# Reordering the opening, the weight sums and the q scalings of a retention and two-layer kernel

## The chip, the cores and the metric

The kernel runs on one core of a Trainium2 chip. The metric is the device time of one execution in microseconds (us).

## The reference

Retention with a decaying state, then two dense layers with an activation between them; the reference, cut to its core:

```python
# B, H, S, D = 4, 8, 768, 64; d_model 512, d_ff 2048
gamma = 1.0 - 2.0 ** (-5.0 - np.arange(H))
for t in range(S):
    state = gamma[None, :, None, None] * state + np.einsum('bhd,bhe->bhde', k[:, :, t], v[:, :, t])
    y[:, :, t] = scale * np.einsum('bhd,bhde->bhe', q[:, :, t], state)
x = y.transpose(0, 2, 1, 3).reshape(B * S, H * D)
h = x @ w_in
out = (h * np.tanh(softplus(h))) @ w_out
```

## The kernel before, in words

**Tiling.** The tokens of each batch are cut into chunks of 128, 24 in all (numbered over the batches). Inside a chunk retention is done by matrix products: scores of k against q, a triangular mask, the masked scores times v, and q times the state that the chunk before left; the state itself is the sum of the outer products of k and v, with a decay. q and v are scaled by powers of gamma when they are turned to fp16 (`qs`, `vs`).

**Blocks.** The dense layers work on blocks of chunks: the first block has four (chunks 0 to 3), each later one two. `first_block` does the retention of chunks 0 to 3 in fp16, whose x goes straight into the first layer (`first_g1` for the first four of 16 groups of d_ff, `g1` for the other twelve), and then calls `first_g2`, the second layer of block 0. `first_g2` also prepares chunks 4 to 7: it scales q and v (`cast_q`, `cast_v` on POOL), loads k as fp16 through POOL's DMA queue (`bring_k`), transposes q and k (`turn` on TensorE for chunks 4 and 5, `turn_by_dma` through SP's DMA queue from chunk 6 on), and does the scores, masks and state of block 1's chunks 4 and 5.

From block 1 on both layers are done with seven products in place of eight (`g1_seven`, `seven`): that needs sums of the weights. `win_sums` makes those of the input weights (`wsum`, two lots `a` of eight DVE additions each), `weight_sums` those of the output weights (`tmat`, two halves of four additions each), `g_sum` those of the activations of block 0 (`gsum`). Weight sums that are not done at once wait in the list `late`; `some_late(n)` issues the next n of them on DVE.

**Weights.** Both weight matrices are loaded as fp32 in four slices each (`wi`, `wt`) and cast to fp16: `cast_win(slice, half, engine)` and `cast_wout`. The table `plan` in `first_block` says after which of the groups 4 to 15 of the first layer which cast or sum is issued. `mish` is the activation, on ACT, which reads a group's PSUM tile and frees it; four of the tiles rotate under the tag `mm` (two others, tag `at`, hold scores, y and groups 8 and 9).

**Order.** The program is written out by hand: each engine runs its instructions in the order of the code, and semaphores hold it until what it reads is there. `gate(x)` is a one-column POOL copy that makes the POOL work behind it wait for x. `steps_of_first` is the table for block 1: what is issued between which of its products.

**Names and lines that the prediction uses.** L249 q of the first chunks; L288 `cast_two` of v on POOL; L204 and L206 `cast_win` on ACT and on POOL or DVE; L214 and L216 `cast_wout` on ACT and DVE; L314 `scores_half`; L321 `mask_half`; L333 `outer_first`; L343 and L345 `state_first` (matmul with the identity, then the multiplication on DVE); L374 `present_first`; L381 `past_first`; L386 `xt_out`; L1057 `first_g1`; L687 `g1`; L703 `mish`; L770 `win_sums`; L722 to L725 `weight_sums`; L406 `cast_q`; L418 `bring_k`; L423 `cast_v`; L427 `gate`; L431 `turn_by_dma`; L453 and L455 `turn`; L604 `outer_fifth`; L614 `decay_of_fifth`; L497 `scores_two`; L1242, L1247 and L1281 copies and additions of outputs in `first_g2`.

Of the kernel before, what the change touches and what calls it, by code (L numbers as in the profile page):

```python
# [11 lines left out]
AF = mybir.ActivationFunctionType  # L12
# [4 lines left out]
def kernel(  # L17
# [125 lines left out]
    nload, late, early = [0], [], set()  # L143
    BRING = CPB
    stores = []
    last_ended, yet = [], []

# [49 lines left out]
    def cast_win(s, half, eng):  # L199
        src = wtmps["in", s]  # L200
        t = cpool.tile([P, NBP, TB // 2], FP16, name=f"win{s}_{half}")
        src = src[:, :, half * (TB // 2):(half + 1) * (TB // 2)]
        if eng is nc.scalar:
            nc.scalar.copy(t, src)  # L204
        else:
            eng.tensor_copy(t, src)  # L206
        wins[s, half] = t
# [190 lines left out]
    def by_head(g, t):  # L398
        if g < NCH:
            return t.rearrange("p (x j) d -> p x j d", x=2)  # L400
        return t.rearrange("p (j x) d -> p x j d", x=2)

    def cast_q(g):
        if g < NCK:
            f = qs.rearrange("p (x j) -> p x j", x=2).unsqueeze(3)
            nc.gpsimd.tensor_tensor(  # L406
                by_head(g, room16(g)[0]), by_head(0, loaded[g][0]),
                f.broadcast_to((P, 2, HP, D)), op=ALU.mult)
# [40 lines left out]
    def turn(g, on_act=False):  # L449
        q16, k16 = cast[g][:2]  # L450
        t_ps = atps.tile([P, H, C], FP16, name="t_ps", tag="at")
        for i in range(HP):
            nc.tensor.transpose(t_ps[:, i], q16[:, 2 * i:2 * i + 2], ident)  # L453
        for i in range(HP):
            nc.tensor.transpose(t_ps[:, HP + i], k16[:, 2 * i:2 * i + 2], ident)  # L455
        qkt = qktp.tile([P, H, C], FP16, name="qkt", bufs=4)
        if on_act:
            nc.scalar.copy(qkt, t_ps)
        else:
            nc.vector.tensor_copy(qkt, t_ps)  # L460
        qkts[g] = (qkt[:, :HP], qkt[:, HP:])
# [599 lines left out]
    def first_block():  # L1061
# [50 lines left out]
        for half in range(2):  # L1112
            cast_two("v", 1, half)
        cast_win(0, 0, nc.gpsimd)
        at = at_tile()
        scores_half(1, 1, at)
        mask_half(1, 1, at)
        y = [atps.tile([P, 2, HP, C], FP32, name="y_ps", tag="at")[:, 0] for _ in range(2)]
        outer_first(1, [0])
        state_first(2)  # L1120
        h_ps = [mmps.tile([P, 1, TB], FP32, name="h_ps", tag="mm") for _ in range(2)]
        for u in range(2):
# [1 line left out]
        present_first(1, y, range(HP))  # L1124
        past_first(2, y)
        past_first(3, y)
        cast_win(0, 1, nc.vector)
        xt_out_by_two(2, y)
        for u in range(2, FPS):
            h_ps.append(mmps.tile([P, 1, TB], FP32, name="h_ps", tag="mm"))  # L1130
# [13 lines left out]

        def more_sums():
            late.extend(win_sums(1))
            some_late(8)
            late.extend(weight_sums(0) + weight_sums(1))

        plan = {6: [(cast_win, NSL - 1, 0, nc.scalar)],  # L1150
                7: [(cast_win, NSL - 1, 1, nc.scalar), (more_sums,)],
                9: [(cast_wout, 0, slice(0, 3)), (cast_wout, 0, slice(3, 4), True), (room_for_more,),
                    (bring_first,)],
                10: [(some_late, 1)],
# [30 lines left out]
    def first_g2():  # L1185
# [33 lines left out]
        for p in pairs:  # L1219
            mm(pe[p], sm(p, 1), t(1), True)  # L1220
            nc.scalar.copy(m5[p], pe[p])
        cast_wout(2, slice(0, 2))
        cast_wout(2, slice(2, 4), True)
        some_late(1)
        gate(tmats[0][:, 1, 0, :1])
        cast_q(CPB)
        cast_q(CPB + 1)
        cast_v(CPB)
        some_late(1)
# [10 lines left out]
        for p in pairs:  # L1240
            mm(px[p], sm(p, 2), t(2))
            nc.scalar.copy(osb[p][0][:, 1], px[p])  # L1242
        mm(pe[0], sm(0, 4), b(2, 1))
        turn(CPB, True)
        for p in pairs:
            mm(px[p], sm(p, 3), t(3))
# [14 lines left out]
        scores(CPB + 1)  # L1261
        mask(CPB)
        mask(CPB + 1)
        some_late(2)
        for p in pairs:
            mm(px[p], a(p, 1, 2), t(4))
        cast_v(CPB + 2)
        bring_k(CPB + 3)
        cast_q(CPB + 2)
        turn_by_dma(CPB + 2)  # L1270
        load_early_v(CPB + 4)

        def end(p, i, half):
            for f in range(2 * half, 2 * half + 2):
# [20 lines left out]
        for p, i in ends:  # L1295
            if (p, i) == (0, 1):
                y_two(1)
            end(p, i, 1)
            if (p, i) == (0, 1):
                midway_of_seventh(CPB + 2)  # L1300
            if p == 0:
                ended(p, i)
            if (p, i) == ends[0]:
                some_late(1)
        x_sums(FIRST, lambda: state_sum(CPB + 2))
        last_ended.extend(ends[2:])
        last_ended.append(ended)
# [54 lines left out]
    def steps_of_first(blk):  # L1362
        a, nb = first[blk] + 4, blk + 1
        A, B = slice(0, FPS), slice(FPS, 2 * FPS)
        return {
            "at1": [(gate_x, blk), (cast_q, a - 1), (decay_next, a - 2), (bring_k, a)],
            "at2": [(turn_by_dma, a - 1), (load_to, a + 2), (cast_v, a - 1), (cast_v, a), (bring_k, a + 1)],
            "at3": [(end_first,), (load_to, a + 3)],
            "at5": [(store, 2), (sums_a, blk, A)],
            "g7": [(sums_a, blk, B)],  # L1370
            "m1": [(scores_and_outer, a - 1), (state_midway, a - 1), (state_sum, a - 1),
                   (decay_next, a - 1)],
            "m5": [(sums_b, blk), (gate_g, blk), (mask_two, nb), (cast_q, a), (turn_by_dma, a),
                   ],
            "m2": [(sums_c, blk), (gate_s, blk), (cast_q, a + 1), (turn_by_dma, a + 1),
                   (load_to, a + 4), (store, 2)],
            "m7": [(y_of, nb), (state_midway, a), (state_sum, a), (decay_next, a)],
            "m3": [(y_end,), (bring_k, a + 2)],
            "m4": [(x_sums, nb)],
        }  # L1380
# [38 lines left out]
```

## Time and profile before

| | us |
|---|---|
| median of 3 runs | 190.89 (190.85 to 191.61) |
| the profiled execution | 190.88 |
| its span in the trace | 189.0 |

The profiled execution's own time is 1.88 us longer than its span: what lies around the first and last instruction. Engines are named PE (TensorE matmul), PEld (its weight loads), DVE (VectorE), ACT (ScalarE), POOL (GpSimd), SP (SyncE, which here only issues DMAs). A row of the timeline has the start and the length in us, the engine, the line of the kernel, the operation, the tile written and the tile read, the size and the number of instructions merged in the row; in brackets, the idle time before it and what ended it. A matmul's end is modelled, and rows of pipelined instructions overlap. The stages by the timeline: the opening with retention of chunks 0 to 3 up to about 20 us, the first layer of block 0 to about 30.6 us, its second layer with the retention of chunks 4 and 5 to about 47 us, then ten blocks of two chunks of some 14 us each, and the last stores.

### The profile page before, as it was taken

What the parts mean: (1) busy time and instruction counts of PE and PEld (TensorE: products, weight loads), DVE (VectorE), ACT (ScalarE), POOL (GpSimd) and SP (SyncE); (2) the same over time, 40 slices, a digit from 0 to 9 for tenths busy, and PEclk for the clock granted to TensorE, in tenths of its full rate; (3) what the DMA queues carried; (4) which work ended last, traced back from release to release, by engine and by line L of the source; (5) the groups of instructions that cost most, each with busy time, mean ns of one, the idle gap of its engine ahead of it and who ended that gap; (6) DMA issues with size and microseconds to landing.
All of it is one profiled execution on the core that took longest, in us unless ns stands there. A gap on an engine that the chain in (4) does not pass through costs nothing.

```text
span 189.0 us, 7724 instructions
## 1 busy us (share of the span) xinstructions
PE 182.5 (97%) x3283; PEld 155.8 (82%) x3283; DVE 155.6 (82%) x329; ACT 126.8 (67%) x249; POOL 95.3 (50%) x135
## 2 busy tenths in 40 slices
PE   7789999999999999999999999999999999999992
PEld 3457546975988988988988988988988989989981
DVE  3997899879899699797897897797897897796662
ACT  3462599385883983983983984974874974965960
POOL 6570107696878937924935925916916913000000
PEclk9999999999999999999999999999999999999999
DMA  5999999999999999999998995999996984300203
GB/s 165 351 368 405 404 407 279 278 248 134 151 192 251 180 285 210 208 219 177 167 194 146 188 187 158 197 195 120 178 203 117 148 144 59 114 0 17 101 0 111
DMA packets 95521, 36.17 MB, mean 191 GB/s; under 512 B 82560, under 2 KB 88960, under 8 KB 95488
## 3 DMA queue, kind: packets, MB, share of 16 engines
q1 hardware_dynamic: 74112, 32.78, 75.3%
q0 software_dynamic: 21088, 2.62, 22.4%
q8 instruction: 25, 0.41, 0.9%
q10 hardware_dynamic: 288, 0.30, 0.4%
q14 instruction: 8, 0.07, 0.1%
HBM read 27.30 MB, written 6.29 MB: 178 GB/s over the span
## 4 chain that ended last, share of the span: by engine, by line
PE 91%; DVE 3%; DMA 2%; POOL 1%; issue 1%; ACT 0%; SPq 0%; DVEq 0%; POOLq 0%
PE h_ps L820 34%; PE o_ps L956 32%; PE h_ps L687 6%; PE o_ps L1210 5%; DMA qfirst<-in_q_dram 2%; PE h_ps L1057 2%; PE o_ps L1275 2%; PE y_ps L532 2%; PE u_ps L483 2%; PE at L497 2%; DVE am L321 2%; PE y_ps L543 2%; POOL qfirst L249 1%; DVE osb L977 1%; PE at L314 0%
## 5 line engine op out<-in xcount | busy, mean ns | idle before, releaser
L840 DVE TENSOR_TENSOR hsum<-h_ps,hsnap 128x512 f32<-128x512 f32 x60 | 38.5, 685 | 10.1 <-ACT hsnap L830 6.6
L830 ACT COPY hsnap<-h_ps 128x512 f32<-128x512 f32 x60 | 32.1, 589 | 10.3 <-PE h_ps L820 10.1
L820 PEld LDWEIGHTS <-wsum 128*128 128x128 f16 x640 | 36.2, 98 | 0.1
L835 ACT ACTIVATE g<-hsum 128x512 f16<-128x512 f32 x60 | 34.6, 643 | 0.6 <-DVE hsum L840 0.2
L956 PEld LDWEIGHTS <-gsum 128*128 128x128 f16 x320 | 30.4, 98 | 3.7
L820 PE MATMUL h_ps<-xsum,wsum 128*128 128x128 f16 x480 | 30.2, 220 | 0.0
L956 PE MATMUL o_ps<-tmat,gsum 128*128 128x256 f16 x240 | 29.5, 273 | 0.0
L820 PEld LDWEIGHTS <-win 128*128 128x128 f16 x480 | 28.2, 98 | 0.9
L418 POOL DMA_DIRECT2D qk<-in_k_dram x36 | 27.5, 777 | 0.0
L956 PEld LDWEIGHTS <-g 128*128 128x128 f16 x248 | 22.7, 98 | 2.6
L406 POOL TENSOR_TENSOR qk<-qf,qvs 128x512 f16<-128x512 f32 x20 | 22.1, 1106 | 0.0
L956 PE MATMUL o_ps<-wout,g 128*128 128x256 f16 (+1 forms) x168 | 20.8, 268 | 0.0
L423 POOL TENSOR_TENSOR v<-vf,qvs 128x512 f16<-128x512 f32 x20 | 20.7, 1060 | 0.0
L820 PE MATMUL h_ps<-xt,win 128*128 128x128 f16 x320 | 19.6, 220 | 0.0
L550 ACT COPY hsum<-y_ps 128x512 f32<-128x512 f32 x9 | 5.3, 585 | 18.3 <-PE y_ps L543 18.3
L977 DVE TENSOR_TENSOR osb<-o_ps,snap 128x256 f32<-128x256 f32 (+1 forms) x32 | 13.0, 413 | 5.0 <-PE o_ps L956 2.4
L597 POOL TENSOR_TENSOR stc<-suc,gcv 128x256 f16<-128x256 f32 x15 | 9.9, 662 | 13.6 <-DVE suc L592 13.6
L427 POOL COPY gate<-gsum 128x1 f16<-128x1 f16 x10 | 1.9, 186 | 26.8 <-DVE gsum L927 26.8
L965 ACT COPY snap<-o_ps 128x256 f32<-128x256 f32 x31 | 11.4, 371 | 5.4 <-PE o_ps L956 5.0
L820 PE MATMUL h_ps<-xsum,win 128*128 128x128 f16 x160 | 12.3, 220 | 0.0
L820 PE MATMUL h_ps<-xt,wsum 128*128 128x128 f16 x160 | 12.2, 220 | 0.0
L835 ACT ACTIVATE g<-h_ps 128x512 f16<-128x512 f32 x20 | 12.0, 599 | 0.0
(144 smaller groups left out, 309.4 us busy)
## 6 DMA issues: line engine op xcount, KB each, us to landing
vf<-in_v_dram SPq DMA_DIRECT2D x24, 256.0 KB, 6.2
out_dram<-osb SPq DMA_DIRECT2D x22, 256.0 KB, 2.9
qf<-in_q_dram SPq DMA_DIRECT2D x20, 256.0 KB, 5.3
wi<-in_moe_w_in_dram SPq DMA_DIRECT2D x3, 1024.0 KB, 10.5
wt<-in_moe_w_out_dram SPq DMA_DIRECT2D x3, 1024.0 KB, 9.6
qk<-in_k_dram POOLq DMA_DIRECT2D x36, 64.0 KB, 5.1
qfirst<-in_q_dram SPq DMA_DIRECT2D x2, 512.0 KB, 4.3
kf<-in_k_dram SPq DMA_DIRECT2D x4, 256.0 KB, 4.9
```

Of the source, the lines that this page charges most:

```text
L406: nc.gpsimd.tensor_tensor(by_head(g, room16(g)[0]), by_head(0, loaded[g][0]), f.broadcast_to((P, 2, HP, D)), op=ALU.mult)
L418: nc.gpsimd.dma_start(room16(g)[1][:, x::2], src[:, HP * x:HP * x + HP])
L423: nc.gpsimd.tensor_tensor(room16(g)[2], loaded[g][2], vs.unsqueeze(2).broadcast_to((P, H, D)), op=ALU.mult)
L597: by.tensor_tensor(stcs[g], sus.pop(g), decay, op=ALU.mult)
L687: nc.tensor.matmul(h_ps[:, j], win(s, f, bp), xt(blk, bp), start=(bp == 0), stop=(bp == NBP - 1))
L820: nc.tensor.matmul(h_ps[g][:, f], w(g, f, d), x(d), start=first and f == 0 and d == 0, stop=d == n - 1, skip_group_check=True)
L830: nc.scalar.copy(x, h_ps)
L835: nc.scalar.activation(gt[:, fb:fb + FPS, j * P:(j + 1) * P], h, AF.Mish, scale=inv_boost3)
L840: nc.vector.tensor_tensor(h, h_ps, x, op=ALU.add)
L956: nc.tensor.matmul(t, x(f), w(f)[:, c], start=first and f == 0, stop=f == n - 1, skip_group_check=True)
L965: nc.scalar.copy(x[:, c], t)
L977: nc.vector.tensor_tensor(dst[:, c], t, plus[:, c], op=ALU.add)
```

## The change

It moves work in time and between engines; no product is added or left out.

- Opening: `outer_first` of chunk 2 stands ahead of the last scores. The second half of input weight slice 0 is cast by POOL, behind the first half, where DVE did it.
- First layer of block 0: the second half of slice 3 is cast by DVE, where ACT did it. Of the last eight additions of `wsum` six are made there; two are kept in a new list `later` and issued in `first_g2`, one behind the third output weight's cast, one ahead of the transposes of chunk 4.
- `first_g2`: the q of chunk 4 is scaled half by ACT (four activations, `cast_q_half`) and half by POOL (`cast_q_rest`). `turn` transposes k ahead of q. The q of chunk 6 stands ahead of the k loads of chunk 7 on POOL, and the q of chunk 7 is scaled right behind these, where block 1 did it behind a gate. The last two additions of `tmat` are issued together, ahead of an output's addition.

```diff
+    def cast_q_half(g):
+        dst, src = by_head(g, room16(g)[0]), by_head(0, loaded[g][0])
+        for j in range(HP // 2):
+            for x in range(2):
+                h = x * HP + j
+                nc.scalar.activation(dst[:, x, j], src[:, x, j], AF.Copy, scale=qs[:, h:h + 1])
+
+    def cast_q_rest(g):
+        f = qs.rearrange("p (x j) -> p x j", x=2)[:, :, HP // 2:].unsqueeze(3)
+        nc.gpsimd.tensor_tensor(
+            by_head(g, room16(g)[0])[:, :, HP // 2:], by_head(0, loaded[g][0])[:, :, HP // 2:],
+            f.broadcast_to((P, 2, HP // 2, D)), op=ALU.mult)
...
         for i in range(HP):
+            nc.tensor.transpose(t_ps[:, HP + i], k16[:, 2 * i:2 * i + 2], ident)
+        for i in range(HP):
             nc.tensor.transpose(t_ps[:, i], q16[:, 2 * i:2 * i + 2], ident)
-        for i in range(HP):
-            nc.tensor.transpose(t_ps[:, HP + i], k16[:, 2 * i:2 * i + 2], ident)
...
         cast_win(0, 0, nc.gpsimd)
+        cast_win(0, 1, nc.gpsimd)
+        outer_first(1, [0])
         at = at_tile()
         scores_half(1, 1, at)
         mask_half(1, 1, at)
         y = [atps.tile([P, 2, HP, C], FP32, name="y_ps", tag="at")[:, 0] for _ in range(2)]
-        outer_first(1, [0])
         state_first(2)
...
-        cast_win(0, 1, nc.vector)
         xt_out_by_two(2, y)
...
             late.extend(win_sums(1))
-            some_late(8)
+            some_late(6)
+            later.extend(late)
+            late.clear()
             late.extend(weight_sums(0) + weight_sums(1))
...
-                7: [(cast_win, NSL - 1, 1, nc.scalar), (more_sums,)],
+                7: [(cast_win, NSL - 1, 1, nc.vector), (more_sums,)],
...
         cast_wout(2, slice(0, 2))
+        later.pop(0)()
         cast_wout(2, slice(2, 4), True)
+        cast_q_half(CPB)
         some_late(1)
         gate(tmats[0][:, 1, 0, :1])
-        cast_q(CPB)
+        cast_q_rest(CPB)
         cast_q(CPB + 1)
...
         mm(pe[0], sm(0, 4), b(2, 1))
+        later.pop(0)()
         turn(CPB, True)
...
-        some_late(2)
+        some_late(3)
         for p in pairs:
             mm(px[p], a(p, 1, 2), t(4))
         cast_v(CPB + 2)
-        bring_k(CPB + 3)
         cast_q(CPB + 2)
         turn_by_dma(CPB + 2)
         load_early_v(CPB + 4)
+        bring_k(CPB + 3)
+        cast_q(CPB + 3)
...
-            if (p, i) == ends[0]:
-                some_late(1)
...
-            "at1": [(gate_x, blk), (cast_q, a - 1), (decay_next, a - 2), (bring_k, a)],
-            "at2": [(turn_by_dma, a - 1), (load_to, a + 2), (cast_v, a - 1), (cast_v, a), (bring_k, a + 1)],
+            "at1": [(turn_by_dma, a - 1), (gate_x, blk), (decay_next, a - 2), (bring_k, a)],
+            "at2": [(load_to, a + 2), (cast_v, a - 1), (cast_v, a), (bring_k, a + 1)],
```

How this stands on the engines, at three places. On ACT, in the first layer of block 0 (`g` is the activation, `win_0_565` and `win_1_573` the two halves of input weight slice 3, `wout` output weights), before:

```order
L703 ACTIVATE g<-h_ps 128x512 x6
L204 COPY win_0_565<-wi 128x1024
L703 ACTIVATE g<-h_ps 128x512
L204 COPY win_1_573<-wi 128x1024
L703 ACTIVATE g<-h_ps 128x512 x2
L214 COPY wout_600<-wt 128x512
L703 ACTIVATE g<-h_ps 128x512 x7
```

and of the change:

```order
L716 ACTIVATE g<-h_ps 128x512 x6
L204 COPY win_0_565<-wi 128x1024
L716 ACTIVATE g<-h_ps 128x512 x3
L214 COPY wout_598<-wt 128x512
L716 ACTIVATE g<-h_ps 128x512 x7
```

The cast of the second half is gone from ACT; three activations now stand together. On DVE, in the second layer of block 0 (the tiles as above), before:

```order
L216 COPY wout_702<-wt 128x1024
L723 TENSOR_TENSOR tmat<-wout_702,tmat 128x1024
L724 TENSOR_TENSOR tmat<-wout_702,wout_600 128x1024
L1183 TENSOR_TENSOR gsum<-g,gsum 128x1024
L725 TENSOR_TENSOR tmat<-wout_702,tmat 128x1024
L1247 TENSOR_TENSOR osb<-o_ps,snap 128x256 x2
```

and of the change:

```order
L216 COPY wout_700<-wt 128x1024
L783 TENSOR_TENSOR wsum<-win_1_515,win_1_573 128x2x256
L736 TENSOR_TENSOR tmat<-wout_700,tmat 128x1024
L737 TENSOR_TENSOR tmat<-wout_700,wout_598 128x1024
L1198 TENSOR_TENSOR gsum<-g,gsum 128x1024
L738 TENSOR_TENSOR tmat<-wout_700,tmat 128x1024
L783 TENSOR_TENSOR wsum<-win_1_515,wsum 128x2x256
L1265 TENSOR_TENSOR osb<-o_ps,snap 128x256 x2
```

The two kept `wsum` additions stand behind the weight cast and ahead of the output additions. On POOL, in the same stage and into block 1 (`qk` is the fp16 tile of a chunk's q and k: 605 or 603 for chunk 4, 608 or 606 for chunk 5, 780 or 784 for chunk 6, 861 or 872 for chunk 7), before:

```order
L427 COPY gate<-tmat 128x1
L406 TENSOR_TENSOR qk_605<-qf,qvs 128x512
L406 TENSOR_TENSOR qk_608<-qf,qvs 128x512
L423 TENSOR_TENSOR v_606<-vf,qvs 128x512
L418 DMA qk_780<-in_k_dram 128x4x64 x2
L423 TENSOR_TENSOR v_609<-vf,qvs 128x512
L423 TENSOR_TENSOR v_781<-vf,qvs 128x512
L418 DMA qk_861<-in_k_dram 128x4x64 x2
L406 TENSOR_TENSOR qk_780<-qf,qvs 128x2x4x64
L427 COPY gate<-xsum 128x1
L406 TENSOR_TENSOR qk_861<-qf,qvs 128x2x4x64
```

and of the change:

```order
L440 COPY gate<-tmat 128x1
L412 TENSOR_TENSOR qk_603<-qf,qvs 128x2x128
L419 TENSOR_TENSOR qk_606<-qf,qvs 128x512
L436 TENSOR_TENSOR v_604<-vf,qvs 128x512
L431 DMA qk_784<-in_k_dram 128x4x64 x2
L436 TENSOR_TENSOR v_607<-vf,qvs 128x512
L436 TENSOR_TENSOR v_785<-vf,qvs 128x512
L419 TENSOR_TENSOR qk_784<-qf,qvs 128x2x4x64
L431 DMA qk_872<-in_k_dram 128x4x64 x2
L419 TENSOR_TENSOR qk_872<-qf,qvs 128x2x4x64
L440 COPY gate<-xsum 128x1
```

The first q scaling is half as wide; the q of chunk 6 and the k loads of chunk 7 have changed places; the q of chunk 7 stands ahead of the gate.

More of the change, by code (lines that the diff above doesn't have):

```diff
@@ L145 @@
     stores = []
-    last_ended, yet = [], []
+    last_ended, yet, later = [], [], []
     def room(g):
```

## The prediction

> **What bounds the kernel now.** I read the page's busy shares and the chain of work that ended last first, then the table of stages, then the timeline of the stages that the diff touches.
>
> ```profile
> span 189.0 us, 7724 instructions
> PE 182.5 (97%) x3283; PEld 155.8 (82%) x3283; DVE 155.6 (82%) x329; ACT 126.8 (67%) x249; POOL 95.3 (50%) x135
> ...
> PE 91%; DVE 3%; DMA 2%; POOL 1%; issue 1%; ACT 0%; SPq 0%; DVEq 0%; POOLq 0%
> ```
>
> TensorE is busy for 97% of the span and is 91% of the chain that ended last. A change of order among the other engines can win only where TensorE waits. The table of stages (length, then busy time and instructions of PE, PEld, DVE, ACT, POOL) says where, among the stages that the diff touches:
>
> ```profile
> 10.00:15.00 5.00, 4.19 (x113) 3.06 (x105) 5.00 (x6) 3.02 (x5) 3.52 (x4) 1.00 1.11 378
> ...
> 25.00:30.50 5.50, 5.46 (x26) 2.40 (x25) 5.34 (x14) 5.50 (x11) 1.62 (x2) 1.00 1.07 392
> 30.50:36.00 5.50, 5.50 (x52) 4.88 (x50) 5.25 (x10) 3.48 (x8) 3.08 (x4) 1.00 1.46 220
> 36.00:42.00 6.00, 6.00 (x80) 5.05 (x79) 4.38 (x6) 4.24 (x6) 5.99 (x7) 1.00 1.08 286
> ```
>
> From 10 to 15 us PE is idle for 0.81 us, from 25 to 30.5 us for 0.04 us (a matmul's end is modelled, so the true stall may be a little more), and from 30.5 to 42 us for none. Most edits lie where there is nothing to win: they can only keep cover or lose it. The granted clock is 1.00 in each of these rows, so it takes no part.
>
> **The change, part by part.** *The outer products ahead of the scores.* The timeline of the opening:
>
> ```profile
> 11.36 2.08 POOL L288 TENSOR_TENSOR v<-vf,qvs 128x512 f16<-128x512 f32 x2 [0.96 <-DMA vf<-in_v_dram]
> ...
> 13.46 1.02 ACT L386 CAST xt<-y_ps 128x1024 f16<-128x1024 f32 x1
> 13.48 1.04 POOL L206 CAST win<-wi 128x1024 f16<-128x1024 f32 x1
> ...
> 13.70 0.42 PE L314 MATMUL at<-qfirst_t,qkt 64*64 64x128 f16 x16 [0.32 <-DVE am L321]
> 14.05 0.62 PE L333 MATMUL u_ps<-v,qk 64*128 64x128 f16 x8
> 14.17 1.22 DVE L321 TENSOR_TENSOR am<-at,tri_first 128x1024 f16<-128x1024 f32 x1
> ...
> 14.60 0.39 PE L343 MATMUL u_ps<-st,ident 128*128 128x512 f16 x1
> ...
> 14.83 1.04 PE L1057 MATMUL h_ps<-xt,win 128*128 128x256 f16 x8
> 15.31 0.68 DVE L345 TENSOR_TENSOR st<-u_ps,gcm 128x512 f16<-128x512 f32 x1
> ...
> 15.80 0.64 PE L374 MATMUL y_ps<-am,v 64*64 64x128 f16 x32
> ...
> 16.37 0.62 PE L381 MATMUL y_ps<-qfirst_t,st 128*128 128x128 f16 x8
> ```
>
> The scores (L314) wait until 13.70 for the mask that frees their PSUM buffer. The outer products (L333) need only v, which POOL has ready at 11.36 + 2.08 = 13.44. Put first, they start at about 13.50 and hold PE for 14.60 - 14.05 = 0.55; the scores follow at 14.05 for 14.05 - 13.70 = 0.35; L343 comes at 14.40 in place of 14.60. That is **0.20 us** sooner. The next readers allow it: L1057, then at 14.63, needs xt (13.46 + 1.02 = 14.48) and the cast weights (13.48 + 1.04 = 14.52). The mask pays: it began 0.47 after the scores, so it begins at 14.52, ends at 15.74, and the state (1.14 after the mask's start) ends at 16.34. The second half of L374, which reads that mask, comes at 15.60 + 0.32 = 15.92, and the second half of L381, which reads that state, at 16.17 + 0.25 = 16.42. Both hold by 0.1 to 0.2 us. Bounds: 0 to 0.3 us (13.70 back to the 0.32 idle, capped by 14.52); I take 0.2, where the rows meet.
>
> *The second half of the first input weights, from DVE to POOL.* It follows the 13.48 cast, once its load has landed:
>
> ```profile
> 8.41 1.43 SPq L184 DMA_DIRECT2D wi<-in_moe_w_in_dram  x2
> ...
> wi<-in_moe_w_in_dram SPq DMA_DIRECT2D x1, 512.0 KB, 5.6
> ```
>
> The second issue, at about 9.1, lands 5.6 us later, at 14.7. With 1.04 for the cast the weights are there at 15.8; their first reader is the third group of L1057, after L381, at about 16.7. Cover 0.9 us, cost nothing. POOL's next work waits for DVE well past that.
>
> *The last half of the fourth input weights, from ACT to DVE, and two weight sums later.* Here PE has its other wait:
>
> ```profile
> 25.28 1.04 ACT L204 CAST win<-wi 128x1024 f16<-128x1024 f32 x1
> ...
> 27.69 1.10 ACT L703 ACTIVATE g<-h_ps 128x512 f16<-128x512 f32 x2
> ...
> 28.84 0.31 PEld L687 LDWEIGHTS <-win 128*128 128x128 f16 x2 [0.32 <-issue]
> ...
> 28.45 0.42 DVE L770 TENSOR_TENSOR wsum<-win,wsum 128x512 f16<-128x512 f16 x1
> 28.79 0.95 DVE L216 CAST wout<-wt 128x1536 f16<-128x1536 f32 x1
> ```
>
> ACT's two activations end at 27.69 + 1.10 = 28.79, and PE's weight load begins at 28.84 after 0.32 idle. Loads in this stage are some 0.22 apart and take 0.10 (two in 0.31), so 0.12 of that is usual and 0.20 is a wait. I read it as the wait of group 14 for the PSUM buffer of group 10, whose activation is the second of these two. Without the 1.04 cast ahead of it that activation ends about 1 us sooner: another **0.20 us** (bounds 0 and 0.32). On DVE one cast is added (0.68, as on DVE elsewhere; 0.95 at the most, by the larger cast above) and two sums leave at 28.79 - 28.45 = 0.34 each: the next step, the cast at 28.79, moves by nothing to +0.27; PE, 0.4 sooner, must not overtake what follows it.
>
> *The stage around the first output product.* The two sums come back here, and POOL's q work is split:
>
> ```profile
> 34.05 0.69 DVE L723 TENSOR_TENSOR tmat<-wout,tmat 128x1024 f16<-128x1024 f16 x1 [0.25 <-ACT wout L214]
> ...
> 34.89 0.50 POOL L427 COPY gate<-tmat 128x1 f16<-128x1 f16 x1 [2.42 <-DVE tmat L723]
> 35.35 2.95 POOL L406 TENSOR_TENSOR qk<-qf,qvs 128x512 f16<-128x512 f32 x2
> 35.87 1.53 DVE L725 TENSOR_TENSOR tmat<-wout,tmat 128x1024 f16<-128x1024 f16 x1
> 36.44 0.81 ACT L1242 COPY osb<-o_ps 128x256 f32<-128x256 f32 x2 [2.42 <-PE o_ps L1210]
> ...
> 37.11 0.39 PE L453 MATMUL t_ps<-ident,qk 128*128 128x128 f16 x4
> ...
> 38.20 0.86 DVE L1247 TENSOR_TENSOR osb<-o_ps,snap 128x256 f32<-128x256 f32 x2 [0.80 <-PE o_ps L1210]
> 38.26 1.04 POOL L423 TENSOR_TENSOR v<-vf,qvs 128x512 f16<-128x512 f32 x1
> ...
> 39.85 0.32 PE L604 MATMUL u_ps<-v,qk 128*64 128x64 f16 x8
> ...
> 42.32 1.06 ACT L614 ACTIVATE stc<-suc,gcf 128x64 f16<-128x64 f32 x4
> ```
>
> ACT's half of q is four 128x64 activations, as L614: 1.06 us within 2.42 idle. POOL's half is half of 1.5 or less. PE, 0.4 sooner, would be at the transposes at 36.71, before q of chunk 4 was ready (35.35 + 1.5 = 36.85); with the split it is ready by about 36.3, and k is turned first. The first late sum (0.34 to 0.42) fills the 0.25 before 34.05, the second the 0.80 before 38.20. ACT's half adds a wait for the load of that q, with the output copies of 36.44 queued behind it: POOL found it landed at 35.35, and if it lands no sooner than that, ACT is done at 36.41 and the copies, wanted at 36.04, are 0.4 late. Cost 0 each, bound +0.4; v of chunk 4, ready at 39.30 against 39.85 - 0.4 = 39.45, has the thinnest cover, 0.15, and POOL's saved 0.5 widens it.
>
> DVE's L725 took 1.53 where the same form took 0.69 at 34.05, beside two POOL scalings of 2.95 together: the two engines held each other up by about 0.8. The Trainium skill ("SBUF — State Buffer", Who interferes with whom) has a rule for it that speaks against this change: a DVE operation with two SBUF inputs and a GpSimd operation that reads SBUF exclude each other for a whole instruction. These rows agree with it. By the rule in its worse order of issue the sum would end at 190.7 to 190.9, as in rival (a); in the better order it stays.
>
> *q of chunks 6 and 7 sooner, the last output weight sum ahead of an output add.* Neither is on PE's path now. SP issues its DMAs in the same order as before; on POOL the q of chunk 6 is moved past the two loads of k of chunk 7 (rival (b) prices that), and the q of chunk 7 past a gate and a state's decay. The sum ahead of the add costs the add 0.6 to 0.93 us; the add frees a PSUM buffer that PE wants some 2 us later. Cost 0, bound +0.2.
>
> The sum: -0.20 - 0.20 = -0.4 us; span 188.6. The profiled execution took 190.88 us, 1.88 around its span, and equals the median of the runs shown (190.89) within 0.01: **190.5 us**.
>
> **The rivals.** *(a) The cover fails and the gain is eaten.* The mask and state of the opening hold by only 0.1, and in the stage from 33 to 40 us DVE and POOL exclude each other: a sum of 0.42 that starts ahead of POOL, or a scaling of about 1 us ahead of a sum, makes v of chunk 4 late by up to 0.4 at 39.45. Either takes back 0.2 to 0.4: 190.7 to 190.9. For it: 1.53 against 0.69. Against it: POOL has 0.5 less to do.
>
> *(b) k of chunk 7 becomes the bound, and the kernel is slower.* On POOL q of chunk 6 now goes ahead of the loads of k of chunk 7, and SP's transpose of chunk 7 waits for these.
>
> ```profile
> 42.80 1.55 POOL L418 DMA_DIRECT2D qk<-in_k_dram  x2
> 44.36 1.17 POOL L406 TENSOR_TENSOR qk<-qf,qvs 128x512 f16<-128x512 f32 x1
> ...
> DMA to landing us min/median/max: 2.8/4.3/6.5
> ...
> qkt<-qk SPq DMA_TRANSPOSE x1, 4.1
> ...
> 53.83 0.43 PE L497 MATMUL at<-qkt 64*64 64x64 f16 x32
> ```
>
> The second k load was issued at about 43.6; 1.17 later, less the 0.5 that POOL saves, is 44.3. It lands 2.8 to 6.5 later, at 47.1 to 50.8, and the transpose 4.1 after that, at 51.2 to 54.9. PE wants it at 53.83 - 0.4 = 53.4. It decides from a landing of 5.0 us on; at 6.5 PE waits 1.5 us: 192.0. Against it: the median landing is 4.3, and the k loads now start when the SP loads ahead are further on.
>
> *(c) More than the sum.* PE's whole idle time in these stages is 0.85, of which the opening's first half is not touched; if both waits go with their full 0.32 and the weight load's usual spacing shrinks too, 190.2.
>
> *(d) The change does not do what it says.* If group 14 waited for something else than ACT, for example its weights, only the opening counts: 190.7.
>
> **How the numbers follow.** Forecast, 190.3 to 190.7 with (d): 0.62. (a), up to 191.1 if both covers fail: 0.24. (b), 192.0: 0.07. (c), 190.0 to 190.3: 0.07. The range takes in the forecast, (a) and most of (c): 190.1 to 191.1. A measurement of this kernel tells about 0.5%, 0.95 us, from no change. Faster by more would need under 189.9, more than the idle time of PE that is touched: 0.02. Slower by more, above 191.8, is (b) and little else: 0.08. Within it: 0.90.
>
> **What would show it.** Right: in the profile after, L333 stands ahead of L314 from about 13.5 us with no PE wait on the mask; PE's first group at 14.6; no idle weight load near 28.8; PE still without idle time from 30 to 60 us; the first seven-product block starts 0.4 us sooner. Wrong: a PE wait on POOL v, on ACT's or POOL's q, on the mask or the state of the opening, or on the transpose of chunk 7 near 53 us; or a DVE sum over 1 us long beside POOL whose reader on PE waits.

## The result and the profile after

The changed kernel takes **192.26 us** (median of eight executions, 191.29 to 192.51), the kernel before, measured beside it, 190.84 us (eight executions, 190.74 to 191.61): a ratio of 1.0059, with a 95% interval of 1.004 to 1.0079. It is slower by about 1.4 us by the medians, where 0.4 us less was forecast; 192.26 lies outside the range of 190.1 to 191.1.

Seven of the eight executions took 192.07 to 192.51 us and one 191.29. The profile of the changed kernel is of that one, so it shows only a part of the loss; a second profile of the same kernel, the first experiment, shows the rest. Its page begins:

```profile
span 189.5 us, 7730 instructions
...
PE 80%; DVE 6%; DMA 6%; SPq 5%; issue 1%; DVEq 0%
```

TensorE's share of the chain has gone from 91% to 80%. That is no measure of a loss: the chain leaves TensorE at its last wait, and everything before this wait is booked under other names, here the casts and loads that led to a wait at 32 us. It tells where to look. The opening and the end of the first layer, on PE and PEld:

```profile
13.30 0.62 PE L333 MATMUL u_ps<-v,qk 64*128 64x128 f16 x8
...
14.58 1.05 PE L1070 MATMUL h_ps<-xt,win 128*128 128x256 f16 x8
...
27.94 1.61 PEld L700 LDWEIGHTS <-win 128*128 128x128 f16 x8
...
30.31 1.04 PE L1225 MATMUL o_ps<-wout,g 128*128 128x256 f16 x8
```

Of the kernel before, the rows that this and the next part are read against, PE and DVE:

```profile
30.56 1.04 PE L1210 MATMUL o_ps<-wout,g 128*128 128x256 f16 x8
...
44.55 0.68 DVE L1281 TENSOR_TENSOR osb<-o_ps,osb 128x512 f32<-128x512 f32 x1
...
46.89 1.95 PE L820 MATMUL h_ps<-xt,win 128*128 128x128 f16 x32
...
52.72 1.04 PE L956 MATMUL o_ps<-wout,g 128*128 128x256 f16 x8
```

Both waits that the change aimed at are gone: L333 runs at 13.30 with no wait ahead of it, the first layer starts at 14.58 (before: 14.83), and the weight loads near 28.8 come in one row of eight without a break. The first product of the second layer starts at 30.31, before at 30.56: **0.25 us gained**. Then it is lost, and more. The next 17 us, PE, DVE and POOL:

```profile
29.66 1.98 POOL L428 DMA_DIRECT2D qk<-in_k_dram  x2
30.99 1.43 DVE L216 CAST wout<-wt 128x1536 f16<-128x1536 f32 x1
31.18 1.04 PE L1225 MATMUL o_ps<-tmat,gsum 128*128 128x256 f16 x8
32.47 1.27 PE L1225 MATMUL o_ps<-wout,g 128*128 128x256 f16 x10 [0.25 <-DVE wout L216]
...
42.99 1.05 POOL L419 TENSOR_TENSOR qk<-qf,qvs 128x512 f16<-128x512 f32 x1
43.56 1.30 DVE L736 TENSOR_TENSOR tmat<-wout,tmat 128x1024 f16<-128x1024 f16 x1
...
45.38 0.68 DVE L738 TENSOR_TENSOR tmat<-wout,tmat 128x1024 f16<-128x1024 f16 x1
45.53 1.42 POOL L419 TENSOR_TENSOR qk<-qf,qvs 128x512 f16<-128x512 f32 x1
45.98 0.68 DVE L1300 TENSOR_TENSOR osb<-o_ps,osb 128x512 f32<-128x512 f32 x1
46.23 1.03 PE L1294 MATMUL o_ps<-wout,g 128*128 128x512 f16 x4
47.10 1.95 PE L833 MATMUL h_ps<-xt,win 128*128 128x128 f16 x32
```

At 32 us TensorE waits for a cast of output weights that took 1.43 us beside POOL's issue of two k loads; the same cast took 0.95 in the kernel before. Eight products before it started at 31.18, the next at 32.47, 1.29 later, where the kernel before needs 0.87 (31.44 to 32.31): 0.42 lost. From the first product of L1225 to the first of L833, block 1's first layer, it is 47.10 - 30.31 = 16.79, before 46.89 - 30.56 = 16.33. A further 0.16 is lost inside that layer (from its first product at 47.10 to the first of its second layer 5.99, before 5.83):

```profile
53.09 1.04 PE L969 MATMUL o_ps<-wout,g 128*128 128x256 f16 x8
```

So -0.25 + 0.46 + 0.16 = +0.37 for this execution, which took 0.41 more than the profiled one of before. The other 1 us of the seven longer executions is not in this profile. What is there is a near miss: three output weight sums (L736 to L738) now stand ahead of the output addition L1300, and the last of them begins at 45.38, 0.15 before POOL's scaling of the q of chunk 7 at 45.53. Here the sum comes up first and takes 0.68, and the scaling is stretched to 1.42.

### The profile page after: what moved, and what is told of

It is laid out like the page before. It is cut to its first block, busy times and chain, and to the rows that moved or that the text cites. A ratio compares the mean times of both kernels' runs of the same rounds, so it can differ in the third digit from the quotient of the medians.

```text
span 189.5 us, 7730 instructions
## 1 busy us (share of the span) xinstructions
PE 183.2 (97%) x3283; PEld 156.1 (82%) x3283; DVE 156.1 (82%) x329; ACT 127.2 (67%) x252; POOL 95.4 (50%) x136
## 4 chain that ended last, share of the span: by engine, by line
PE 80%; DVE 6%; DMA 6%; SPq 5%; issue 1%; DVEq 0%
PE h_ps L833 34%; PE o_ps L969 32%; DMA wi<-in_moe_w_in_dram 6%; PE o_ps L1225 4%; SPq L270 3%; DVE wsum L783 3%; PE o_ps L1294 2%; PE y_ps L545 2%; PE at L510 2%; PE u_ps L496 2%; PE y_ps L556 2%; DVE wout L216 1%; SPq L184 1%; DVE win L206 1%; DVE osb L990 1%
## 5 line engine op out<-in xcount | busy, mean ns | idle before, releaser
L833 PEld LDWEIGHTS <-wsum 128*128 128x128 f16 x640 | 36.2, 98 | 0.1
L833 PE MATMUL h_ps<-xsum,wsum 128*128 128x128 f16 x480 | 30.1, 219 | 0.0
L833 PEld LDWEIGHTS <-win 128*128 128x128 f16 x480 | 28.2, 98 | 0.9
L419 POOL TENSOR_TENSOR qk<-qf,qvs 128x512 f16<-128x512 f32 x19 | 20.9, 1098 | 0.0
L833 PE MATMUL h_ps<-xt,win 128*128 128x128 f16 x320 | 19.6, 219 | 0.0
L833 PE MATMUL h_ps<-xsum,win 128*128 128x128 f16 x160 | 12.3, 220 | 0.0
L833 PE MATMUL h_ps<-xt,wsum 128*128 128x128 f16 x160 | 12.2, 219 | 0.0
```

The costliest lines, as they stand in the source:

```text
L419: nc.gpsimd.tensor_tensor(by_head(g, room16(g)[0]), by_head(0, loaded[g][0]), f.broadcast_to((P, 2, HP, D)), op=ALU.mult)
L833: nc.tensor.matmul(h_ps[g][:, f], w(g, f, d), x(d), start=first and f == 0 and d == 0, stop=d == n - 1, skip_group_check=True)
```

## The experiments

Three explanations were tried. **The pair:** the output weight sums, now all ahead of an output addition, meet the q scalings of chunks 6 and 7, now beside them on POOL; the sums are held, the addition comes late, and TensorE, which needs that addition's PSUM buffer, waits at 47 us. **The cast:** the loss is the cast at 31 us and what follows on VectorE. **The k loads:** the k of chunk 7 is late, rival (b) of the prediction. The runs are told in the order of the argument, each by what its kernel is against the changed kernel or, where that is shorter, against the kernel before.

For all runs, from the profiled execution of each: where the first product of block 0's second layer starts, and how long this stage lasts, to the first product of block 1 (us).

| kernel | starts at | stage | median (range, executions) | before, measured beside it | ratio (95%) |
|---|---|---|---|---|---|
| before | 30.56 | 16.33 | 190.84 (190.74-191.61, 8) | | |
| changed | 30.31 | 16.79 | 192.26 (191.29-192.51, 8) | 190.84 | 1.0059 (1.004-1.0079) |
| changed, again | 30.31 | 17.73 | 193.26 (1) | 191.1 | |
| opening back | 30.38 | 17.69 | 192.22 (191.21-193.59, 12) | 191.1 | 1.0046 (1.0022-1.007) |
| casts and sums back | 30.61 | 16.99 | 192.05 (191.36-192.71, 12) | 191.1 | 1.0028 (1.0004-1.0052) |
| q order back | 30.30 | 16.80 | 191.43 (191.17-192.74, 12) | 191.1 | 1.0007 (0.9982-1.0032) |
| sum behind the addition | 31.10 | 17.10 | 191.68 (191.33-192.77, 12) | 191.45 | 1.0023 (1.0006-1.004) |
| q of chunk 7 back | 30.30 | 16.74 | 191.46 (191.13-194.85, 12) | 191.45 | 1.001 (0.9988-1.0033) |
| k loads early | 30.27 | 16.70 | 192.77 (192.06-193.23, 8) | 191.45 | 1.0073 (1.0049-1.0097) |
| only q order and sum | 30.64 | 17.10 | 191.98 (191.11-192.33, 12) | 191.45 | 1.0021 (0.9998-1.0044) |
| opening, cast, split | 30.41 | 16.90 | 191.81 (191.43-193.41, 12) | 191.41 | 1.0032 (1.0007-1.0058) |
| opening, cast | 30.35 | 17.01 | 191.58 (191.23-193.22, 12) | 191.41 | 1.0016 (0.9991-1.0041) |
| q order without sum | 30.28 | 16.90 | 191.59 (191.47-194.12, 12) | 191.41 | 1.0032 (1.0002-1.0063) |

The kernel before has a median of 190.84 to 191.45 from one set of executions to another, with a lowest time of 190.66 to 190.83; of its longer sets each has executions of over 192 us too. Its stage lengths are those of one execution. Times are compared within a set. The start of the second layer can differ by 0.08 us without any edit: the kernel before and the one with only the q order and the sum are the same program up to there, and have 30.56 and 30.64.

### The changed kernel again

No edit; one execution, for its profile.

> The changed kernel once more, for a second profile: the one at hand is of its fastest execution (191.29 us), while most took 192.1 to 192.5. Theory L (VectorE's cast of the second output weight at about 31 us is held up by GpSimd's issue of the k loads, and TensorE waits for it): the profile shows a cast of over 1.3 us there and TensorE idle by 0.4 to 1.4 us just after it; a time near 192.3 goes with the longer wait. Rival K (the k loads of chunk 7 are late and their transpose holds TensorE near 53 us): at 192.3 the wait shows there, up to 1.5 us, and none over 0.5 us at 32 us.

193.26 us. It shows the wait that the first profile lacks. DVE, POOL and PE:

```profile
43.56 1.77 DVE L736 TENSOR_TENSOR tmat<-wout,tmat 128x1024 f16<-128x1024 f16 x1
...
45.53 1.30 POOL L419 TENSOR_TENSOR qk<-qf,qvs 128x512 f16<-128x512 f32 x1
45.86 1.52 DVE L738 TENSOR_TENSOR tmat<-wout,tmat 128x1024 f16<-128x1024 f16 x1
47.31 0.68 DVE L1300 TENSOR_TENSOR osb<-o_ps,osb 128x512 f32<-128x512 f32 x1
...
48.04 1.96 PE L833 MATMUL h_ps<-xt,win 128*128 128x128 f16 x32 [0.78 <-DVE osb L1300]
```

Now L738 comes up at 45.86, after the scaling has begun at 45.53, and takes 1.52 where it took 0.68. It comes up later because the first sum, L736, took 1.77 from the same start at 43.56, and not 1.30. The addition starts at 47.31, before the change at 44.55; TensorE gets its buffer at 48.04, where it was due at 47.10: 0.94 lost. With the 191.29 of the shortest execution that gives 192.23, the median within 0.03. So of two executions of one program the one in which the last sum begins 0.15 us ahead of the scaling, and not 0.33 behind it, is faster here by the 0.94. The seven longer executions of the result have no profile of their own; that they have this wait is inferred from their times, and from the next run. (The rest of the 193.26 is a wait in a later block, whose code the diff doesn't touch, for a transpose by DMA:

```profile
84.42 0.32 PE L510 MATMUL at<-qkt 64*64 64x64 f16 x16 [0.86 <-DMA qkt<-qk]
```

It stands in three of the thirteen profiles, this one, that of the q of chunk 7 back with 1.76 and that of the opening and cast with 0.48. The one profile of the kernel before doesn't have it, which doesn't say that no execution of it does.)

### Opening back

```diff
-        cast_win(0, 1, nc.gpsimd)
-        outer_first(1, [0])
         at = at_tile()
...
+        outer_first(1, [0])
         state_first(2)
...
+        cast_win(0, 1, nc.vector)
         xt_out_by_two(2, y)
```

> The change without its opening: outer products behind the scores again, second half of input weight 0 on VectorE again. Theory L: TensorE comes to the second output weight 0.2 to 0.3 us later, so the wait for the cast shrinks by as much and no more; 191.0 to 192.3, no faster than the kernel before. Rival O (the opening itself sets off the slow executions, by the casts on GpSimd): back to 190.5 to 190.9. Rival K: unchanged, 192.3.

192.22: the loss is all there without the opening's edits. Its second layer starts at 30.38, the changed kernel's at 30.31: beside the other edits, the opening is worth 0.07 us, which is no more than the start differs without an edit. The profile, of an execution at the median (192.27), shows two waits:

```profile
34.84 2.04 POOL L440 COPY gate<-tmat 128x1 f16<-128x1 f16 x1 [2.41 <-DVE tmat L736]
...
37.15 0.69 PE L468 MATMUL t_ps<-ident,qk 128*128 128x128 f16 x4
37.68 1.04 PE L1225 MATMUL o_ps<-tmat,gsum 128*128 128x256 f16 x8
...
45.89 1.53 DVE L738 TENSOR_TENSOR tmat<-wout,tmat 128x1024 f16<-128x1024 f16 x1
47.33 0.68 DVE L1300 TENSOR_TENSOR osb<-o_ps,osb 128x512 f32<-128x512 f32 x1
48.07 1.96 PE L833 MATMUL h_ps<-xt,win 128*128 128x128 f16 x32 [0.90 <-DVE osb L1300]
```

The one at 47 is that of the pair. The other is new: the gate, a copy of one column, takes 2.04 us (0.50 in the kernel before), and ends with VectorE's sums, which run back to back from 33.67 to 36.83. The second half of the q of chunk 4 comes from POOL at 37.45, and the four transposes that read it take 0.53 to the next product instead of 0.22: 0.31 lost. In this profile the cast at 30.99 took 0.96 and the k loads' issue 2.76, so there is no wait at 32.

### Casts and sums back

```diff
-                7: [(cast_win, NSL - 1, 1, nc.vector), (more_sums,)],
+                7: [(cast_win, NSL - 1, 1, nc.scalar), (more_sums,)],
```

with all eight `wsum` additions at their old place.

> The change with the second half of input weight 3 on ScalarE again and all eight weight sums in the first layer, none later. Theory L: VectorE's cast falls at another moment against the k loads; the first layer's 0.2 us wait for ScalarE comes back; 190.6 to 191.2 if the cast escapes the loads, 192.3 if it doesn't. Rival K: unchanged, 192.3.

192.05. Without the cast on VectorE and the late sums, the gate takes 0.50 again and the cast at 31.05 takes 0.95: neither wait, at 32 or at 37, is there. The wait at 47 is:

```profile
44.90 2.05 DVE L738 TENSOR_TENSOR tmat<-wout,tmat 128x1024 f16<-128x1024 f16 x1
45.32 1.06 POOL L419 TENSOR_TENSOR qk<-qf,qvs 128x512 f16<-128x512 f32 x1
46.87 0.68 DVE L1296 TENSOR_TENSOR osb<-o_ps,osb 128x512 f32<-128x512 f32 x1
47.60 1.57 PE L833 MATMUL h_ps<-xt,win 128*128 128x128 f16 x25 [0.50 <-DVE osb L1296]
```

So the cast is not the main cause. Here L738 begins at 44.90, 0.42 ahead of the scaling, and is held all the same: it comes up while POOL still issues the k loads (43.77 to 45.32). So it is not only a matter of which of the two starts first. And the second layer starts at 30.61: with the opening changed but ACT's cast in its old place, the opening's gain is gone before it gets there.

### q order back

```diff
+        bring_k(CPB + 3)
         cast_q(CPB + 2)
         turn_by_dma(CPB + 2)
         load_early_v(CPB + 4)
-        bring_k(CPB + 3)
-        cast_q(CPB + 3)
...
-            "at1": [(turn_by_dma, a - 1), (gate_x, blk), ...
+            "at1": [(gate_x, blk), (cast_q, a - 1), ...
...
```

> The change with the q of chunk 6 behind the k loads of chunk 7 again and the q of chunk 7 and its transpose behind block 1's gate again. Theory L: no change, 192.0 to 192.5. Rival K: the loss goes, 190.5 to 191.3.

191.43 against 191.1, a ratio of 1.0007 (0.9982 to 1.0032), shortest 191.17: within the interval the loss is gone; what is left by the medians, 0.33, is about what the shortest execution of the changed kernel showed. DVE, POOL and PE:

```profile
43.56 0.68 DVE L736 TENSOR_TENSOR tmat<-wout,tmat 128x1024 f16<-128x1024 f16 x1
...
44.52 1.22 POOL L419 TENSOR_TENSOR qk<-qf,qvs 128x512 f16<-128x512 f32 x1
44.76 1.53 DVE L738 TENSOR_TENSOR tmat<-wout,tmat 128x1024 f16<-128x1024 f16 x1
46.21 0.68 DVE L1299 TENSOR_TENSOR osb<-o_ps,osb 128x512 f32<-128x512 f32 x1
47.10 1.95 PE L833 MATMUL h_ps<-xt,win 128*128 128x128 f16 x32
```

L738 is held here too, 1.53, by the scaling of chunk 6. But only once: the addition starts 1.1 us earlier than in the second profile of the changed kernel, and TensorE does not wait.

### Sum behind the addition, and q of chunk 7 back

The first of these two takes the last `tmat` addition alone back behind the output's addition, the second the q of chunk 7 (with its transpose) alone back into block 1.

```diff
-        some_late(3)
+        some_late(2)
...
+            if (p, i) == ends[0]:
+                some_late(1)
```

> The change with the last output weight sum behind the output addition again, as before; all else changed. Theory P (near 44 to 47 us VectorE's weight sums wait while GpSimd scales q of chunks 6 and 7; with the last sum ahead of the output addition, that addition, which frees TensorE's PSUM buffer for block 1, is late): the addition starts by 45.5 us whatever the sums take, TensorE's wait at 47 us (0.7 to 1.1 us in the slow executions) is gone, time 191.0 to 191.5, no 192.3. Rival K (late k loads of chunk 7): unchanged. Rival Q (the q order alone is enough): the wait at 47 us stays, 192.3.

```diff
         bring_k(CPB + 3)
-        cast_q(CPB + 3)
...
-            "at1": [(turn_by_dma, a - 1), (gate_x, blk), ...
+            "at1": [(gate_x, blk), (cast_q, a - 1), ...
...
```

> The change with only the q of chunk 7 and its transpose back behind block 1's gate; q of chunk 6 stays ahead of the k loads of chunk 7, the sum stays ahead of the addition. Theory P: the sum behind q of chunk 6 still takes 1.2 to 1.9 us, the last sum 0.7, the addition starts at 46.0 to 46.7, TensorE waits at 47 us for 0 to 0.3 us: 191.0 to 191.6. If the issue of the k loads is what holds the sums: both stay long and TensorE waits 0.7 to 1.1 us, 192.3.

191.68 and 191.46, with 191.45 for the kernel before beside them; the changed kernel itself was 1.4 above the kernel before in its own set. The first keeps a small loss (its interval, 1.0006 to 1.004, lies above 1), the second none that can be told. Either half of the pair taken away removes the wait at 47. Both profiles were disturbed elsewhere (a wait of 0.85 us at 15 us for input weights that landed late in the one, the wait of 1.76 us at 84 us in the other), but the place itself can be read. In the second, the sums run on without the scaling of chunk 7, and TensorE starts without a wait:

```profile
45.15 0.68 DVE L738 TENSOR_TENSOR tmat<-wout,tmat 128x1024 f16<-128x1024 f16 x1
45.75 0.68 DVE L1299 TENSOR_TENSOR osb<-o_ps,osb 128x512 f32<-128x512 f32 x1
```

### Only the q order and the sum

The kernel before with these two edits alone.

```diff
-        some_late(2)
+        some_late(3)
...
         cast_v(CPB + 2)
-        bring_k(CPB + 3)
         cast_q(CPB + 2)
...
+        bring_k(CPB + 3)
+        cast_q(CPB + 3)
...
```

> The kernel before with two parts alone: q of chunks 6 and 7 sooner, and the last sum ahead of the addition. Theory P: these two make the loss; the wait at 47 us is there with 0.6 to 1.2 us, 191.6 to 192.1, about 1 us over the kernel before; no wait at 32 us. Rival: the loss needs the changed opening or the late sums; 190.8 to 191.0.

191.98 against 191.45; eleven of the twelve executions took 191.84 to 192.33, one 191.11, again two groups. The ratio's interval (0.9998 to 1.0044) just takes in 1, so the time alone doesn't settle it; the profile, of an execution at the median (192.00), does. The pair alone makes the wait:

```profile
45.04 2.04 DVE L738 TENSOR_TENSOR tmat<-wout,tmat 128x1024 f16<-128x1024 f16 x1
45.46 1.06 POOL L419 TENSOR_TENSOR qk<-qf,qvs 128x512 f16<-128x512 f32 x1
47.00 0.68 DVE L1295 TENSOR_TENSOR osb<-o_ps,osb 128x512 f32<-128x512 f32 x1
47.74 1.46 PE L833 MATMUL h_ps<-xt,win 128*128 128x128 f16 x23 [0.60 <-DVE osb L1295]
```

By the pace of the six products ahead of it (45.66, six at 0.217) L833 was due at 46.96: 0.78 lost. The second layer starts at 30.64, as in the run without the cast on VectorE (30.61, with the opening changed): the opening alone brings the start of the second layer 0.03 us, nothing that can be told from one profile each.

### The k loads early

To take the cast's partner away, the k loads of chunks 4 and 5 are issued earlier on POOL; the sum stands behind the addition, as above, so that the pair is out of the way.

```diff
-        gate(wtmps["out", 1][:, 0, :1])
+        gate(wtmps["out", 0][:, 0, :1])
```

> As the run with the sum behind the addition, and the gate ahead of the k loads of chunks 4 and 5 waits for the first output weight in place of the second, so they are issued at about 26.5 us. Theory L (their issue holds VectorE's cast of the second output weight): the cast at 31 us takes 0.95, TensorE's 0.4 us wait at 32 us goes, 190.4 to 190.8, faster than the kernel before by 0.1 to 0.4 us. Rival: the cast is long for another reason, or the loads then delay the weights; 191.0 or more.

192.77: it missed. The k loads are issued at 26.83, the cast at 30.96 takes 0.95 and the wait at 32 is gone, as expected. That POOL's issue was what held the cast fits, but isn't shown by this: the cast took 0.95 or 0.96 beside that issue in five other profiles too. The rest comes out worse. The gate takes 2.04 and TensorE loses 0.37 at 37 us, and POOL, waiting for a load, comes to its scalings later, beside other sums:

```profile
42.75 1.04 POOL L436 TENSOR_TENSOR v<-vf,qvs 128x512 f16<-128x512 f32 x1 [0.75 <-DMA vf<-in_v_dram]
...
44.27 1.52 DVE L737 TENSOR_TENSOR tmat<-wout,wout 128x1024 f16<-128x1024 f16 x1
...
49.07 0.61 PE L833 MATMUL h_ps<-xt,win 128*128 128x128 f16 x8 [0.43 <-DVE suc L605]
```

The wait at 49 us is for work that stands on VectorE behind the held sums.

### What is left of the gain

Three kernels drop the costly parts and keep those that won. All have the `wsum` additions together and the last `tmat` addition behind the output's addition; the first and second have the old q order too, the second also the q of chunk 4 whole on POOL and the transposes' old order.

```diff
-            some_late(6)
-            later.extend(late)
-            late.clear()
+            some_late(8)
...
-        some_late(3)
+        some_late(2)
...
```

> Of the change this keeps the opening, the cast of the last input weight's second half on VectorE and the split q of chunk 4; the eight input-weight sums stand together again, the q order of chunks 6 and 7 and the place of the output weight sum are as before. If the losses are the three places at which a VectorE instruction and a GpSimd one share the port, the wait at 47 us is gone, GpSimd's gate before the q of chunk 4 takes 0.50 us and not 2.04, and what is left of the gain is 0.2 + 0.2 - 0.2 (the small gap at 52 us): 190.4 to 190.8, or 0.4 more if the cast near 31 us takes 1.43 us. If the loss belongs to the opening or the cast themselves, it stays at 191.3 or more.

> As the run before, and the q of chunk 4 whole on GpSimd and the transposes' order of q and k as before. With the port as the cause the q of chunk 4 holds VectorE's last output weight sum before 36 us as it did in the kernel before (1.53 us), at no cost to TensorE: 190.4 to 190.8, the same as with the split. If the split earns something by itself, this one is 0.2 or more slower than the run before.

> As the first of these three, but with the q of chunks 6 and 7 in the changed order. If only the pair of edits (q order and sum ahead of the add) costs, this is the same as the first within 0.2 us. If the q order costs by itself too (the first output add of block 1, or the 47 us wait), it is 0.3 or more slower, with the output add of block 1's start at 47 us or later.

191.81, 191.58 and 191.59, with 191.41 before: none is faster than the kernel before (the intervals of the first and the third lie above 1), and the expected 190.4 to 190.8 was missed. The gate takes 0.50 in all three, and there is no wait at 47 in the first and the third. But the two additions that now stand ahead of the output weights' casts make VectorE late (first kernel; PE and DVE):

```profile
30.45 0.69 DVE L735 TENSOR_TENSOR tmat<-wout 128x1024 f16<-128x1024 f16 x1
31.06 0.69 DVE L1190 TENSOR_TENSOR gsum<-g 128x1024 f16<-128x1024 f16 x1
31.81 1.05 PE L1223 MATMUL o_ps<-tmat,gsum 128*128 128x256 f16 x8 [0.35 <-DVE gsum L1190]
```

L735 starts at 30.45, before the change at 29.83: the cast that ACT gave up costs VectorE 0.62. (In the changed kernel, where the two sums come later, it starts at 29.78.) TensorE takes 1.40 for eight products (30.41 to 31.81), 0.52 more than before (30.56 to 31.44). So the two sums had to move if VectorE was to take the cast; and each of the seven profiles in which they are moved has the wait at 32 or the one at 37, though by what link isn't shown. In each arrangement tried, the stage gives back 0.37 or more of a gain of at most 0.3. The split q of chunk 4 and the q order without the sum show no cost or gain beyond the intervals.

The second kernel's profile, of its longest execution (193.22), shows one thing more, on POOL and DVE:

```profile
43.48 1.56 POOL L431 DMA_DIRECT2D qk<-in_k_dram  x2
43.71 1.55 DVE L736 TENSOR_TENSOR tmat<-wout,tmat 128x1024 f16<-128x1024 f16 x1
```

No scaling runs beside this sum until 45.04; it takes 1.55, and not 0.68, beside POOL's issue of the k loads alone. So the scalings are not all that holds the sums. No version was found that beats the kernel before.

## Why the prediction was wrong

**The step that failed** is the last of the parts, on the q of chunks 6 and 7 and the last output weight sum: "The sum ahead of the add costs the add 0.6 to 0.93 us; the add frees a PSUM buffer that PE wants some 2 us later. Cost 0, bound +0.2." The sum was priced by its duration in the kernel before, at a place where POOL was about to go idle. The other edit of the same step puts the scaling of chunk 6 and the k loads' issue beside the first of the sums, and the scaling of chunk 7 beside the last. In the second profile of the changed kernel L736 takes 1.77 and L738 1.52; the addition starts at 47.31 and not at 44.55, 2.76 later: more than the some 2 us of cover. Cost 0.94 us for TensorE, where 0 was forecast and 0.2 was the bound. Taking back either edit removes the wait and the two alone make it, so this is shown. What isn't: how many of the eight executions have it (by their times, seven), and what makes the first sum, L736, last 1.30 in one execution and 1.77 in another, by which the last sum meets the scaling or escapes it; POOL issues the k loads just then. The row that should have warned, 1.53 beside POOL against 0.69 alone, was in the prediction, but was used for another stage. Two edits that are each free at this place were costed apart; their price is in the meeting.

The other steps:

- *The outer products ahead of the scores, -0.20.* Right at the place (0.25 sooner at the first layer), wrong in the sum: with the cast moved too, they bring the second layer 0.07 sooner. Most of the gain is gone long before: the 48 products of the later groups (L700) start at 19.94, before (L687) at 20.00, so 0.06 is left there. The 24 products of L1070 ahead of them take 3.02 from 16.62 on, where they took 2.87 from 16.83 on; what holds them isn't shown. And where ACT keeps its cast, nothing of the opening reaches the second layer: its start follows ACT's first cast of the fourth input weights, which waits for their load, by 6.72 or 6.73 in all three profiles (23.84 and 30.56 before, 23.88 and 30.61 with casts and sums back, 23.92 and 30.64 with only the q order and the sum).
- *The second half of the first input weights to POOL, 0.* Right: it is cast at 14.85 and TensorE does not wait for it in the profile after.
- *The last half of the fourth input weights to VectorE, -0.20.* Right: the wait of the weight loads is gone and the start of the second layer is 0.18 sooner by this part without the opening (30.56 to 30.38). Together with the opening 0.25, forecast 0.40; nearly all of the missing 0.15 is the opening's.
- *The late sums and the split q, 0, bound +0.4.* The size was at the edge of the bound, the value wrong: 0.42 at 32 us or 0.31 to 0.38 at 37 us, one or the other in each profile that has the late sums and the moved cast, except that the one with late input weights had both. Rival (a) had the mechanism (VectorE and POOL holding each other up), at 33 to 40 us and by up to 0.4, and 190.7 to 190.9; it had not the cast beside the k loads' issue, nor the place at 47 that decides. The rule of the Trainium skill cited there ("SBUF — State Buffer", Who interferes with whom) named the right danger, and the sums and scalings that met bear it out: a sum held by a scaling alone ended 0.55 or 0.56 us after it, a held scaling 0.89 or 0.90 after the sum. It isn't the whole: the sum of 1.55 beside the issue of k loads alone had no scaling to wait for.
- *Rival (b), the k of chunk 7, 192.0.* The time is near the result, the mechanism is not there. Block 1's scores at L510 start at 54.20 without a wait on the transposes:

```profile
54.20 0.55 PE L510 MATMUL at<-qkt 64*64 64x64 f16 x32
```

- *Rivals (c) and (d)* did not come: the edits did what they say, and brought no more than the sum.

The chances followed from this: 0.08 for slower rested on rival (b) and little else, since the pair was bounded at +0.2.

**What stays open:** the 0.16 to 0.2 us inside block 1's first layer, at 52 us. They are in every variant and not in the profile of before, also in kernels that share no edit (only the q order and the sum; opening, cast and split), so that no single edit explains them. What holds TensorE's products between 16.6 and 19.6 us, where most of the opening's gain goes. When the issue of k loads holds a sum: in the q of chunk 7 back, two sums ran at 0.68 beside it. And what decides whether the gate slips in between two sums (0.50) or waits for the last (2.04): it took 0.50 behind back-to-back sums too, in the kernel before.

## What to carry to other kernels

When two edits move work of different engines to the same microseconds, look up what each instruction costs beside the other, not what it cost where it stood; ask for each reader's cover against that price. A gain early in a stage counts only as far as it reaches the stage's end: follow it to the last wait there, and ask whether that wait's end is set by something that the gain doesn't move, as here by a load. Where an order is decided by a few tenths of a microsecond, as with the sum and the scaling at 45.5 us, one profile can be of the rarer case: compare its own time with the median before you read it as the kernel.

## What the runs showed of the hardware

- A VectorE sum of two fp16 tiles of 128x1024 and a GpSimd scaling of 128x512 held each other up wherever they met between 33 and 50 us. The sum takes 0.68 alone and up to 2.05 us, the scaling 1.04 alone and up to 1.54. In the thirteen profiles a sum that came up behind a scaling ended 0.55 or 0.56 after it 34 times (the 1.52 of the second profile: 47.38, the scaling 46.83), and 0.82 to 1.34 after it five times, each time L736 with an issue of k loads just behind the scaling. A scaling that came up while a sum ran ended 0.89 or 0.90 after the sum 23 times (the 1.42 of the first profile).
- GpSimd's issue of two DMAs can hold such a sum too: 1.55 beside the issue alone (the opening and the cast). In the q of chunk 7 back, two sums ran at 0.68 beside it. A sum that began beside the issue, 0.42 ahead of the scaling, took 2.04 or 2.05, until 0.56 after the scaling (only the q order and the sum; casts and sums back); one that began so 0.15 ahead took 0.68 (the changed kernel). What decides isn't known.
- GpSimd's issue of the k loads of chunks 4 and 5 and VectorE's cast of 128x1536 at 31 us took 1.98 and 1.43 in three profiles, 2.75 or 2.76 and 0.95 or 0.96 in five others, from nearly the same starts.
- The one-column copy on GpSimd that gates the q of chunk 4 took 0.50 us in nine profiles and 2.04 us in four, where it ended when VectorE's row of sums did.
